# Reading three quarters of unit 0's turned rows during the MLP, and loading the output weights later

## The chip, the cores and the metric

The kernel runs on one core of a Trainium2 chip. The metric is the device time of one execution in microseconds, as the median of several runs. All matrices are fp32; products that need accuracy are made of two fp32r parts, a high one and a low one. Engine names below are those of the profile: PE (TensorE matmuls), PEld (its weight loads), DVE (VectorE), ACT (ScalarE), POOL (GpSimd) and SP (SyncE, which here only issues DMAs).

## The reference

One sequence of S = 2048 tokens, width D = 448, is normalised; attention with 16 heads of 28 and one shared key and value head, and a GELU MLP of width 1792, both work on the normalised rows, and both are added to the input:

```python
xn = _layernorm(x, axis=-1)
# attention
q = (xn @ wq).reshape(B, S, H, Dh).transpose(0, 2, 1, 3); k = xn @ wk; v = xn @ wv
p = softmax(einsum("bhqd,bkd->bhqk", q, k) * Dh ** -0.5)
a = einsum("bhqk,bkd->bhqd", p, v).transpose(0, 2, 1, 3).reshape(B, S, H * Dh) @ wo
# MLP, with a layernorm of its own
h = gelu(einsum("bsd,df->bsf", _layernorm(xn), w1) + b1)
return x + a + einsum("bsf,fd->bsd", h, w2) + b2
```

## The kernel before

The schedule is written out by hand: every engine runs its instructions in the order in which the Python code issues them, and the tile framework adds the waits. Three stages follow each other.

**Projections** (to about 64 us). The tokens are worked in four chunks of 512. Each chunk's normalised and transposed rows stand in two tiles of 128 x 2048, the *row buffers*: `xh` (the high part, pool `xt_p`, three buffers) and `xl` (the low part, pool `xl_p`, three buffers).

**MLP** (64 to 481 us). 56 slots: four chunks (`c`, in the order 1, 2, 3, 0) by 14 blocks of F (`ft`). A slot takes some 7.4 us. Between the MLP's products PE also makes score products, three PSUM banks in turn (`mtile`), of two kinds:

- the *max stream* (L598): scores whose row maxima DVE takes (L599);
- the *turned scores* (L632): for one head of each unit, DVE scales and copies the scores of 128 queries into one of two `raw` buffers (L633), ACT takes the exponential (L650), and SP stores the quarter of a head with four DMAs of 256 KB to DRAM, `td<-raw` (L653). The next but one quarter can be written into the same `raw` buffer only when those four DMAs have landed.

**Attention** (481 us to the end). 16 units (512 queries by four heads), each of 8 steps of two key blocks `kt`. Three heads of a unit go by `score` (a product L1037, then the exponential on ACT, L1038). The fourth is the turned one: its rows come back from DRAM by `load_d` (L830, `half<-td`), a *half* tile being 8 key blocks, 256 columns, brought by four DMAs of 32 partitions each; `turn_blocks` (L1013) then turns two key blocks at a time with one DVE transpose of 128 x 1024. The products with the values are `pv` (L999). The strings in `ORDERS` set the order within two steps: `s` a score, `m` a product of the max stream, `t` a turned score, `x` an exponential of turned scores with its stores, `T` a transpose of turned rows, a digit that many `pv`. `begin(n)` stands at the head of step n: it issues the loads for the next unit (`load_d(u + 1, kt // 2)` on SP, `load_q` on POOL).

Unit 0's turned rows are 16 key blocks, four quarters of four. Quarter 0 is read in the MLP's last chunk into a free `xh` row buffer called `ahead` (L788, one DMA of 256 KB in each of the slots 6 to 9). Quarter 1 (L1079, four DMAs of 256 KB) and quarters 2 and 3 (L1081, four DMAs of 512 KB) are issued at the start of the attention stage, behind the four DMAs of the output weights `wor` (L853). These weights are set to zero by POOL (L850), loaded, and split into `woh` (ACT, L856) and `wol` (POOL, L857) by `prep_wo` in steps 4 to 7. They are used by `o_jobs` (L874 to L876) from 674 us on, and `wor` itself at the very end (L950). All three stand in the pool `att`, which is opened when the MLP's pools are closed.

SP issues in order: a DMA that waits (for an engine, or for the eighth DMA before it) holds all that stand behind it.

Of the kernel before, what the change touches and what calls it, by code (L numbers as in the profile page):

```python
# [10 lines left out]
F32 = mybir.dt.float32  # L11
# [31 lines left out]
def block_kernel(ctx, tc, x, wq, wk, wv, wo, w1, b1, w2, b2, out):  # L43
# [4 lines left out]
    def f(t):  # L48
        return t.bitcast(F32)
# [5 lines left out]
    dram = ctx.enter_context(tc.tile_pool(name="dram", bufs=1, space=bass.MemoryType.DRAM))  # L55
    xt_p = ctx.enter_context(tc.tile_pool(name="xt", bufs=len(KEPT)))
    qmp = ctx.enter_context(tc.tile_pool(name="qmp", bufs=1))

    def heads_of(u):
        return 4 - sum(v == u for v, _ in TURNED)  # L60
# [11 lines left out]
    ident = keep.tile([P, P], F32, name="ident")  # L72

    ph1 = ExitStack()
    xl_p = ph1.enter_context(tc.tile_pool(name="xl", bufs=len(KEPT)))
    wp = ph1.enter_context(tc.tile_pool(name="wp", bufs=1))
    lnp = wp.tile([P, NT, 2], F32, name="lnp")
    lnrq = wp.tile([P, 2, NT], F32, name="lnrq")
# [488 lines left out]
        qst.append(xt_p.tile([P, 4, CW], F32R, name="xh"))  # L567
        pool.memset(f(qst[-1]), 0.0)

    qst = []  # L570

    mrs = {}

# [191 lines left out]
    for n in range(len(mslots) + 2):  # L765
        c, ft = mslots[n] if n < len(mslots) else (NCH, n - len(mslots))
        if 3 <= ft < 11 and ft % 2 and len(KEPT) <= c + 1 < NCH:
            line(CT * MLP_ORDER[c + 1] + (ft - 3) // 2)
        k = ft - (10 if c < NCH - 1 else 5)
        if c < NCH and 0 <= k < CT:  # L770
            line(CT * MLP_ORDER[c] + k)
        if c < NCH and 0 < k <= CT:
            a = lines[CT * MLP_ORDER[c] + k - 1]
            pool.tensor_add(a, a, b2b)
        if ft == 0 and 0 < c < NCH:
            a = lines[CT * MLP_ORDER[c - 1] + CT - 1]
            pool.tensor_add(a, a, b2b)
        if (c, ft) == (NCH - 1, 4):
            clear_q()
        if c == NCH - 1 and 6 <= ft < 10:  # L780
            load_q(0, (ft - 6,))
        if (c, ft) == (NCH - 1, 11):
            load_max(0)
        if (c, ft) == (NCH - 1, 5):
            ahead = f(xt_p.tile([P, 4, CW], F32R, name="xh")).rearrange("p b n -> p (b n)").rearrange("p (t k) -> p t k", k=P)
        if c == NCH - 1 and 6 <= ft < 10:
            r = ft - 6
            nc.sync.dma_start(ahead[32 * r:32 * r + 32], td[0, 3][:, r, :, 0:P])  # L788
        ts, pace = 0, 21
        if n == 2:  # L790
            pace = 20
        if 0 < c < NCH:
            pace += {1: -2, 2: -2, 4: 2, 6: 2}.get(ft, 0)
        if n >= len(mslots):
            done = 0
        for _ in slot(n):
            done += 1
            owed += pace
            if n >= len(mslots) and (done % 2 if ft == 0 else done <= 2):
                maxed += mxs.step()  # L800
            elif 0 < n < len(mslots) and owed // 46 > (owed - pace) // 46:
                if n == 1 and ts == 0:
                    ts += tq.step()
                elif ts < 4 and n < len(mslots) - 1 and not split(c, ft):
                    ts += tq.step()
                else:
                    maxed += mxs.step()
        if n == 0:
            for _ in range(3):
                tq.step()  # L810
# [5 lines left out]
    op = ctx.enter_context(tc.tile_pool(name="op", bufs=1, space=PSUM))  # L816
    free_at.update((i, k) for k, i in enumerate((0, 1, 6, 3, 2, 4, 5)))

    wor = att.tile([P, NG, D], F32, name="wor", bufs=1)
    halves = {}  # L820

    def load_d(u, i, at=slice(0, 256)):
        assert stored[u, 3] == CT - 1
        h, r = divmod(i, 4)
        if (u, 3, h) not in halves:
            halves[u, 3, h] = att.tile([P, 4 * CT, 256], F32, name="half", bufs=3)
        part = halves[u, 3, h][32 * r:32 * r + 32]
        if u:
            dve.memset(part[0:1, 0, 0:1], 0.0)
        nc.sync.dma_start(part[:, :, at], td[u, 3][:, r, :, 256 * h + at.start:256 * h + at.stop])  # L830
# [14 lines left out]
        part = part[32 * r:32 * r + 32]  # L845
        nc.sync.dma_start(part, td[u, j][:, r, :, P * q:P * q + P])

    woh = att.tile([P, NG, D], F32R, name="woh", bufs=1)
    wol = att.tile([P, NG, D], F32R, name="wol", bufs=1)
    pool.memset(wor, 0.0)  # L850
    for j in range(4):
        src = wo.rearrange("(g j d) n -> j d g n", j=4, d=DH)[j]
        nc.sync.dma_start(wor[32 * j + 1:32 * j + 1 + DH, :, :], src)  # L853

    def prep_wo(g):
        act.activation(woh[:, g, :], wor[:, g, :], AF.Copy)  # L856
        pool.tensor_sub(wol[:, g, :], wor[:, g, :], f(woh[:, g, :]))  # L857

# [148 lines left out]

    def turn_blocks(u, kt, j):
        p = pair_of()
        part, k = (halves[u, j, kt // 8], kt % 8) if j == 3 else (halves[u, j, kt // 4], kt % 4)  # L1010
        if u == 0 and kt < 4:
            part = ahead
        dve.transpose(p.rearrange("p k (g j) -> p g k j", j=32),  # L1013
                      part[:, :, 32 * k:32 * k + 64].rearrange("p g (k j) -> p g k j", j=32))
        ps[u, kt, j], ps[u, kt + 1, j] = p[:, 0], p[:, 1]
        taken[id(p), 0], taken[id(p), 1] = (u, kt), (u, kt + 1)
# [39 lines left out]
    def begin(n):  # L1056
# [13 lines left out]
        if u == NU - 1 and kt < 4:  # L1070
            for r in range(4):
                load_second(2 + kt // 2, r)
        if 4 <= n < 4 + NG:
            prep_wo(n - 4)
        if u + 1 < NU and kt < 8:
            load_q(u + 1, (kt // 2,))

    for i in range(4):
        load_d(0, i, slice(P, 2 * P))  # L1079
    for i in range(4, 8):  # L1080
        load_d(0, i)  # L1081
    for n0 in range(0, len(steps), 2):
        u, kt0 = steps[n0]
        n, kt = n0, kt0
# [78 lines left out]
```

## Time and profile before

| what | us |
|---|---|
| median of 3 runs (lowest to highest) | 1078.3 (1077.69 to 1078.35) |
| the profiled execution | 1077.61 |
| its span, first to last instruction | 1075.8 |
| PE busy | 1058.8 (98%) |
| DVE, ACT, POOL busy | 914.1 (85%), 723.9 (67%), 563.2 (52%) |
| mean granted TensorE clock | 0.996 |
| moved by DMA | 209.86 MB, mean 195 GB/s |

The lines quoted in the prediction come from these views. *Windows* give for stretches of the span the busy time of each engine with its number of instructions, then the granted TensorE clock (1.00 is full), the busy share of the 16 DMA engines (it can exceed 1) and the GB/s moved. *Timeline* rows have start, duration, engine, line, operation and tiles; a bracket at the end is the idle time of that engine before the row and what ended it. The *chain* is the work that ended last, followed back from a stretch's end: start, duration, what. *Waits* give who waited for whom: total, times, longest. *DMA issues* give count and size of each.

### The profile page before, as it was taken

To read this page: it belongs to the slowest core of one execution; us is meant where nothing else is said; L and a number is where in the kernel's file an instruction comes from. 1 tells how busy PE (TensorE), PEld (TensorE's weight loads), DVE (VectorE), ACT (ScalarE), POOL (GpSimd) and SP (SyncE) were. 2 spreads that over 40 slices of the span, in tenths; PEclk is the share of its full clock that TensorE was granted. 3 is DMA by queue.
4 is the path that set the end of the run, shared out by engine and by line. 5 is a ranking of instruction groups with operands and counts; after the bars stand their busy time and mean duration, and the time that the engine had idled before them with its cause. 6 is when DMAs were issued, how large, how long until landed. Compare 5 with 4: busy or idle time off the path is not lost.

```text
span 1075.8 us, 17796 instructions
## 1 busy us (share of the span) xinstructions
PE 1058.8 (98%) x5805; PEld 714.2 (66%) x5805; DVE 914.1 (85%) x1880; ACT 723.9 (67%) x1240; POOL 563.2 (52%) x704
## 2 busy tenths in 40 slices
PE   9999999999999999998899999999999999999998
PEld 8778888888888888884445455655545644556455
DVE  7889999999999999996788888788888787776755
ACT  6775456565566656545778888678887687775773
POOL 6678787768766777773333434335333335343130
PEclk9999999999999999999999999999999999999999
DMA  8865556668776777859999999999999797896892
GB/s 266 249 220 149 136 133 167 160 169 202 189 188 168 183 190 211 222 142 218 234 221 217 236 211 245 215 191 236 220 227 239 188 222 175 170 189 150 185 213 57
DMA packets 158768, 209.86 MB, mean 195 GB/s; under 512 B 17950, under 2 KB 110276, under 8 KB 158676
## 3 DMA queue, kind: packets, MB, share of 16 engines
q1 hardware_dynamic: 146132, 187.28, 71.7%
q0 software_dynamic: 11136, 20.87, 9.3%
q8 instruction: 46, 0.75, 0.3%
q10 hardware_dynamic: 1408, 0.57, 0.2%
q14 instruction: 46, 0.38, 0.1%
HBM read 121.31 MB, written 86.10 MB: 193 GB/s over the span
## 4 chain that ended last, share of the span: by engine, by line
PE 93%; DMA 2%; DVE 2%; ACT 2%; issue 1%; SPq 0%; POOL 0%; ACTq 0%; DVEq 0%; POOLq 0%
PE po L999 19%; PE m L1037 17%; PE m L598 16%; PE m L715 12%; PE ph L192 11%; PE m L632 6%; PE qp L192 3%; PE ph L195 1%; PE m L874 1%; PE ph L197 1%; PE m L876 1%; PE m L875 1%; DMA half<-td 1%; DMA td<-raw 1%; ACT p L1038 1%; PE po L982 1%
## 5 line engine op out<-in xcount | busy, mean ns | idle before, releaser
L599 DVE TENSOR_REDUCE mx<-m 128x1 f32<-128x512 f32 x752 | 484.7, 682 | 73.7 <-PE m L598 69.7
L1038 ACT ACTIVATE p<-m 128x512 f32<-128x512 f32 x652 | 342.4, 623 | 112.2 <-PE m L1037 109.4
L598 PE MATMUL m<-ks,qm 128*128 128x512 f32 x752 | 289.4, 400 | 4.1 <-DVE raw L633 3.0
L1037 PE MATMUL m<-xh,ks 128*128 128x512 f32 x752 | 261.4, 416 | 4.8 <-DVE mx L599 4.3
L999 PE MATMUL po<-p,vs 128*32 128x512 f32 x1664 | 219.5, 595 | 0.9 <-DVE p L1013 0.9
L1037 PEld LDWEIGHTS m<-xh,ks 128*128 128x128 f32 x752 | 139.1, 189 | 100.9 <-issue 40.8
L633 DVE TENSOR_SCALAR_CACHE_REDUCE raw<-m 128x512 f32<-128x512 f32 x272 | 181.7, 687 | 12.7 <-PE m L632 6.1
L598 PEld LDWEIGHTS m<-ks,qm 128*128 128x128 f32 x752 | 141.9, 189 | 43.8 <-issue 11.7
L650 ACT ACTIVATE raw<-raw,m 128x1024 f32<-128x1024 f32 x136 | 153.0, 1163 | 0.0
L680 ACT ACTIVATE hx<-ph,b1t 128x512 f32<-128x512 f32 x55 | 37.9, 688 | 150.5 <-PE ph L197 98.9
L1013 DVE STREAM_TRANSPOSE p<-half 128x1024 f32<-128x1024 f32 x112 | 137.8, 1234 | 1.5 <-DMA half<-td 1.1
L999 PEld LDWEIGHTS po<-p,vs 128*32 128x32 f32 x1664 | 55.0, 109 | 108.7 <-issue 105.3
L632 PE MATMUL m<-ks,q 128*128 128x512 f32 x272 | 108.1, 398 | 0.1
L696 POOL TENSOR_TENSOR hl<-hx,hh 128x512 fp32r<-128x512 f32 x56 | 72.7, 1298 | 32.4 <-ACT hh L694 32.3
L715 PE MATMUL m<-w2h,hl 128*128 128x448 f32 x224 | 81.4, 367 | 0.0
L715 PE MATMUL m<-w2h,hh 128*128 128x448 f32 x224 | 81.3, 366 | 0.0
L715 PE MATMUL m<-w2l,hh 128*128 128x448 f32 x224 | 81.2, 366 | 0.0
L684 POOL TENSOR_TENSOR hz<-hz,hx 128x512 f32<-128x512 f32 x56 | 72.8, 1300 | 4.6
L689 POOL TENSOR_TENSOR hx<-hx,hz 128x512 f32<-128x512 f32 x56 | 72.7, 1297 | 4.7
L1038 ACT ACTIVATE xh<-m 128x512 f32<-128x512 f32 x100 | 55.9, 624 | 21.5 <-PE m L1037 21.0
L192 PE MATMUL ph<-xh,w1h 128*128 128x512 f32 x165 | 64.7, 392 | 0.0
L999 PE MATMUL po<-xh,vs 128*32 128x512 f32 x256 | 64.7, 595 | 0.0
(197 smaller groups left out, 1499.7 us busy)
## 6 DMA issues: line engine op xcount, KB each, us to landing
td<-raw SPq DMA_DIRECT2D x272, 256.0 KB
half<-td SPq DMA_DIRECT2D x124, 512.0 KB
xh<-qd POOLq DMA_DIRECT2D x56, 168.0 KB, 6.9
qd<-qe SPq DMA_DIRECT2D x24, 256.0 KB
a<-in_A_x_dram SPq DMA_DIRECT2D x24, 224.0 KB
qm<-qd SPq DMA_DIRECT2D x96, 56.0 KB
qm<-qd POOLq DMA_DIRECT2D x92, 56.0 KB, 5.8
ad<-a SPq DMA_DIRECT2D x16, 224.0 KB
```

Source lines behind the costliest of these rows:

```text
L192: pe.matmul(ps, w, v, start=(n == 0), stop=False)
L598: pe.matmul(pm, qm[:, t * P:(t + 1) * P], ks[:, n * CW:(n + 1) * CW], start=True, stop=True)
L599: dve.tensor_reduce(mx[:, CT * j + t, n:n + 1], pm, axis=AX.X, op=ALU.max)
L632: pe.matmul(sc, q3[i % 2][:, t * P:(t + 1) * P], ks[:, n * CW:(n + 1) * CW], start=True, stop=True)
L633: dve.tensor_scalar(raw[:, :, 4 * n:4 * n + 4, :].rearrange("p r b i -> p b r i"), sc.rearrange("p (b r i) -> p b r i", r=4, i=32), SCALE, ...
L650: act.activation(raw[:, rs], raw[:, rs], AF.Exp, bias=m3[:, 4:5], scale=1.0)
L684: pool.tensor_mul(hz, hz, hx)
L715: pe.matmul(m2[k], h[:, k * P:(k + 1) * P], w[:, ft, :], start=(ft == 0 and i == 0), stop=(ft == NF - 1 and i == 2))
L999: pe.matmul(po[32 * j:32 * j + 32, :], vs[:, kt, :], ps.pop((u, kt, j)), start=(kt == 0), stop=(kt == NT - 1))
L1013: dve.transpose(p.rearrange("p k (g j) -> p g k j", j=32), part[:, :, 32 * k:32 * k + 64].rearrange("p g (k j) -> p g k j", j=32))
L1037: pe.matmul(s, ks[:, kt * P:(kt + 1) * P], qss[u][:, j, :], start=True, stop=True)
L1038: act.activation(p, s, AF.Exp, scale=SCALE)
```

## The change

- The pool of `xl` row buffers is opened at the top, so it lives to the end; the pool of the MLP's weights and others after it move up in memory accordingly.
- `ahead` becomes a list of three row buffers, one `xh` and two `xl`, for quarters 0, 1 and 2 of unit 0's turned rows. They are read by twelve DMAs of 256 KB, two in each of the slots 6 to 11 of the MLP's last chunk.
- At the start of the attention stage only quarter 3 is left to read (four DMAs of 256 KB).
- `wor`, `woh`, `wol` are `xl` row buffers. `wor`'s four loads are issued one each in steps 4 to 7; the split is in steps 10 to 13.

```diff
+    xl_p = ctx.enter_context(tc.tile_pool(name="xl", bufs=len(KEPT)))
...
-    xl_p = ph1.enter_context(tc.tile_pool(name="xl", bufs=len(KEPT)))
...
         if (c, ft) == (NCH - 1, 5):
-            ahead = f(xt_p.tile([P, 4, CW], F32R, name="xh")).rearrange("p b n -> p (b n)").rearrange("p (t k) -> p t k", k=P)
-        if c == NCH - 1 and 6 <= ft < 10:
-            r = ft - 6
-            nc.sync.dma_start(ahead[32 * r:32 * r + 32], td[0, 3][:, r, :, 0:P])
+            for p, name in ((xt_p, "xh"), (xl_p, "xl"), (xl_p, "xl")):
+                t = f(p.tile([P, 4, CW], F32R, name=name)).rearrange("p b n -> p (b n)")
+                ahead.append(t.rearrange("p (t k) -> p t k", k=P))
+        if c == NCH - 1 and 6 <= ft < 12:
+            for i in (2 * ft - 12, 2 * ft - 11):
+                q, r = divmod(i, 4)
+                nc.sync.dma_start(ahead[q][32 * r:32 * r + 32], td[0, 3][:, r, :, P * q:P * q + P])
...
-    wor = att.tile([P, NG, D], F32, name="wor", bufs=1)
+    def weights_tile():
+        t = xl_p.tile([P, 4, CW], F32R, name="xl").rearrange("p b n -> p (b n)")
+        return t[:, 0:NG * D].rearrange("p (g d) -> p g d", g=NG)
+
+    wor = f(weights_tile())
...
-    woh = att.tile([P, NG, D], F32R, name="woh", bufs=1)
-    wol = att.tile([P, NG, D], F32R, name="wol", bufs=1)
     pool.memset(wor, 0.0)
-    for j in range(4):
+    woh = wol = None
+
+    def load_wo(j):
         src = wo.rearrange("(g j d) n -> j d g n", j=4, d=DH)[j]
         nc.sync.dma_start(wor[32 * j + 1:32 * j + 1 + DH, :, :], src)
 
     def prep_wo(g):
+        nonlocal woh, wol
+        if g == 0:
+            woh, wol = weights_tile(), weights_tile()
...
-        part, k = (halves[u, j, kt // 8], kt % 8) if j == 3 else (halves[u, j, kt // 4], kt % 4)
-        if u == 0 and kt < 4:
-            part = ahead
+        if u == 0 and kt < 12:
+            part, k = ahead[kt // 4], kt % 4
+        elif j == 3:
+            part, k = halves[u, j, kt // 8], kt % 8
+        else:
+            part, k = halves[u, j, kt // 4], kt % 4
...
-        if 4 <= n < 4 + NG:
-            prep_wo(n - 4)
+        if 4 <= n < 8:
+            load_wo(n - 4)
+        if 10 <= n < 10 + NG:
+            prep_wo(n - 10)
...
-    for i in range(4):
+    for i in range(4, 8):
         load_d(0, i, slice(P, 2 * P))
-    for i in range(4, 8):
-        load_d(0, i)
```

PE's and DVE's instructions stand in the same order as before; SP's, POOL's and ACT's differ. On SP, in the slots 9 to 11 of the MLP's last chunk, before (`xh<-qd` is unit 0's queries, `q` and `qm` queries for coming scores, `mn` unit 0's maxima):

```order
L563 DMA xh<-qd_90 28x3x512
L788 DMA xh<-td_3_73 32x16x128
L498 DMA q_162<-qd_90 28x512 x2
L498 DMA q_162<-qd_91 28x512 x2
L653 DMA td_3_84<-raw 128x1x512 x8
L498 DMA qm_161<-qd_90 28x512 x2
L498 DMA qm_161<-qd_91 28x512 x2
L585 DMA xh<-mn 1x12x128
L586 DMA xh<-mn 1x12x128
L653 DMA td_3_84<-raw 128x1x512 x8
```

And now:

```order
L563 DMA xh<-qd_94 28x3x512
L791 DMA xl<-td_3_76 32x16x128 x2
L498 DMA q_162<-qd_93 28x512 x2
L498 DMA q_162<-qd_94 28x512 x2
L653 DMA td_3_87<-raw 128x1x512 x4
L791 DMA xl<-td_3_76 32x16x128 x2
L653 DMA td_3_87<-raw 128x1x512 x4
L498 DMA qm_161<-qd_93 28x512 x2
L498 DMA qm_161<-qd_94 28x512 x2
L585 DMA xh<-mn 1x12x128
L586 DMA xh<-mn 1x12x128
L791 DMA xl<-td_3_76 32x16x128 x2
```

Each pair of new reads stands ahead of the four (in the last case eight) stores of turned scores of its slot. In the slots 6 to 9 one read became two, in 10 and 11 none became two.

On SP at the start of the attention stage, before:

```order
L721 DMA ad<-a 128x448 x4
L853 DMA wor<-in_A_wo_dram 28x4x448 x4
L830 DMA half<-td_3_73 32x16x128 x4
L830 DMA half<-td_3_73 32x16x256 x4
L830 DMA half<-td_3_74 32x16x256 x7
L653 DMA td_3_85<-raw 128x1x512 x4
```

And now (`xl<-in_A_wo_dram` are the output weights; `td_3_76` is unit 0's turned head, `td_3_77` unit 1's):

```order
L721 DMA ad<-a 128x448 x4
L837 DMA half<-td_3_76 32x16x128 x4
L837 DMA half<-td_3_77 32x16x256 x5
L860 DMA xl<-in_A_wo_dram 28x4x448
L837 DMA half<-td_3_77 32x16x256
L860 DMA xl<-in_A_wo_dram 28x4x448
L837 DMA half<-td_3_77 32x16x256
L860 DMA xl<-in_A_wo_dram 28x4x448
L653 DMA td_3_88<-raw 128x1x512 x4
```

Ahead of the first store of turned scores of this stage there stood 4 weight loads, 4 reads of 256 KB and 11 of 512 KB; now 3 weight loads, 4 reads of 256 KB and 7 of 512 KB.

On DVE, unit 0's second and third transposes (`xh` as a source is quarter 0's row buffer, `xh` as a target a spare one for the turned result), before and now:

```order
L1013 STREAM_TRANSPOSE p<-xh 128x16x2x32
L829 MEMSET half 1x1
L599 TENSOR_REDUCE mx<-m_5705 128x1
L1013 STREAM_TRANSPOSE xh<-half 128x16x2x32
L599 TENSOR_REDUCE mx<-m_5712 128x1
```

```order
L1026 STREAM_TRANSPOSE p<-xh 128x16x2x32
L836 MEMSET half 1x1
L599 TENSOR_REDUCE mx<-m_5703 128x1
L1026 STREAM_TRANSPOSE xh<-xl 128x16x2x32
L599 TENSOR_REDUCE mx<-m_5710 128x1
```

The third transpose stands at the same place and reads a row buffer that the MLP's last chunk filled, where it read a half tile that the attention stage's first DMAs fill.

More of the change, by code (lines that the diff above doesn't have):

```diff
@@ L568, in clear_q @@
         pool.memset(f(qst[-1]), 0.0)
-    qst = []
+    qst, ahead = [], []
     mrs = {}
```

## The prediction

> **What bounds the kernel now.** I read the windows first, to see in which stage PE is not busy.
>
> ```profile
> 66.00:421.00 355.00, 353.91 (x1604) 298.17 (x1603) 339.65 (x742) 209.55 (x292) 268.86 (x263) 1.00 0.66 169
> 421.00:450.00 29.00, 29.00 (x134) 24.74 (x133) 27.43 (x63) 16.85 (x24) 23.17 (x23) 1.00 0.87 247
> 450.00:481.00 31.00, 31.00 (x144) 26.45 (x143) 30.16 (x60) 14.49 (x21) 21.33 (x21) 1.00 0.52 127
> 481.00:545.00 64.00, 55.25 (x291) 29.17 (x289) 47.04 (x94) 44.38 (x85) 22.52 (x32) 0.95 1.08 232
> 545.00:1030.00 485.00, 485.00 (x2912) 257.81 (x2912) 392.55 (x757) 371.94 (x701) 177.48 (x288) 1.00 0.92 207
> ```
>
> The columns after the stretch are PE, PEld, DVE, ACT, POOL, the clock, the DMA share and GB/s. PE is the bound everywhere but in the first 64 us of attention: there it is idle for 64 - 55.25 = 8.75 us and its mean clock falls to 0.95, with the DMA engines at 1.08. The timeline of PE has these gaps:
>
> ```profile
> 481.97 0.50 PE L1037 MATMUL m<-xh,ks 128*128 128x512 f32 x1 [0.49 <-DVE half L829]
> 488.90 1.90 PE L999 MATMUL po<-p,vs 128*32 128x512 f32 x10 [0.88 <-DVE p L1013]
> 500.01 0.73 PE L1037 MATMUL m<-xh,ks 128*128 128x512 f32 x2 [4.28 <-DVE mx L599]
> 531.45 0.70 PE L598 MATMUL m<-ks,qm 128*128 128x512 f32 x1 [2.99 <-DVE raw L633]
> ```
>
> They add up to 8.64 us, so these four are the whole story. DVE's timeline says what DVE itself waited for ahead of the two large ones:
>
> ```profile
> 498.13 1.25 DVE L1013 STREAM_TRANSPOSE xh<-half 128x1024 f32<-128x1024 f32 x1 [5.93 <-DMA half<-td]
> 530.69 0.69 DVE L633 TENSOR_SCALAR_CACHE_REDUCE raw<-m 128x512 f32<-128x512 f32 x1 [3.35 <-DMA td<-raw]
> ```
>
> The first is unit 0's third transpose, which waits for quarter 1; while DVE stands, it frees no PSUM bank, and PE runs out of banks. The second is a turned score that waits until its `raw` buffer has been stored. Narrow windows show what follows a gap:
>
> ```profile
> 486.00:496.00 10.00, 8.86 (x48) 3.34 (x47) 5.32 (x9) 5.29 (x12) 1.50 (x4) 1.00 1.11 210
> 496.00:500.00 4.00, 0.00 (x0) 0.00 (x0) 1.82 (x2) 0.00 (x0) 0.30 (x1) 1.00 1.14 216
> 500.00:505.00 5.00, 4.88 (x13) 3.65 (x14) 4.50 (x12) 3.53 (x7) 3.73 (x8) 0.66 1.13 221
> ...
> 531.00:536.00 5.00, 4.55 (x13) 3.46 (x13) 4.90 (x10) 2.83 (x6) 0.88 (x2) 0.66 1.09 182
> ```
>
> After each large gap the clock is 0.66 over 5 us, so PE loses 5 x 0.34 = 1.70 us more; after the gaps of 0.49 and 0.88 it is full (1.00 in 486 to 496). And the DMA engines are saturated at 210 to 221 GB/s. The chain names the two DMAs that ended last:
>
> ```profile
> 485.96 12.00 DMA half<-td
> ...
> 515.83 1.03 ACT raw L650
> ...
> 519.39 11.11 DMA td<-raw
> ```
>
> A read of 256 KB took 12.00 us and a store of 256 KB 11.11 us, because of what is queued ahead of them.
>
> **The change, part by part.** *The first gap.* Quarter 1 is now in a row buffer that was filled in the MLP, so the third transpose follows the second at once (about 492 instead of 498.13). That returns 4.28 + 1.70 = **5.98 us**. Late next is DVE: between its wait and PE's next value products it has up to 4.5 us of work in 5 us (the row of 500 to 505), while PE's 4.88 us there shrink to 3.2 at full clock. Since DVE then starts 5.93 us earlier, it has that much lead, and I allow 0.4 us for what PE may still wait (between 0, if the lead lasts, and 1.3, the difference 4.5 - 3.2).
>
> *The second gap.* The first store of the attention stage had 4 weight loads (196 KB), 4 reads of 256 KB and 11 of 512 KB ahead of it on SP, 7.62 MB; now it has 3, 4 and 7, 5.32 MB. At 221 GB/s the 2.30 MB less are 10.4 us of queue. But all of it also happens 5.98 us earlier, so that the queue has less time to drain. Rows for the time that is left:
>
> ```profile
> 516.89 3.75 SPq L653 DMA_DIRECT2D td<-raw  x4
> xh<-qd POOLq DMA_DIRECT2D x56, 168.0 KB, 6.9
> ```
>
> In the attention stage a load of 168 KB takes 6.9 us to land (median); I take this for a store in an ordinary queue. The last store (issued at 519.39) took 11.11, 4.2 us more; 4.2 + 5.98 = 10.2 us of queue have to go, and 10.4 go. The store would then land 2.5 (from the first issue, 516.89, to the last) + 6.9 = 9.4 us after the exponential; DVE comes for the buffer at 530.69 - 3.35 = 527.34, which is 10.48 us after the exponential's end at 516.86, and both shift alike. It fits by 1.1 us, so I count the gap as gone: 2.99 + 1.70 = **4.69 us**, between 0 (the queue is no shorter when it counts) and 4.69. That the steady stretch from 545 on runs with PE at 485.00 of 485.00 under the same stores and reads of 512 KB speaks for the upper end.
>
> On the clock, the Trainium skill ("TensorE: Matmul & The Clock Gate", section "What's actually happening") puts the return to half rate after an idle window of about 3.4 us. By it the gap of 2.99 would have left the clock alone, and this term would be 2.99; the row of 531 to 536 shows 0.66, and the row decides.
>
> *The gaps of 0.49 and 0.88* stand in front of any moved data (quarter 0 was already early). I keep them; if POOL's earlier `memset` freed them, 1.37 us more would go.
>
> *The eight added reads in the MLP's last chunk* (twelve now, four before), in stretches of about a slot:
>
> ```profile
> 421.00:428.00 7.00, 7.00 (x34) 5.98 (x33) 6.64 (x16) 3.92 (x6) 5.84 (x6) 1.00 0.89 255
> 428.00:435.00 7.00, 7.00 (x34) 5.96 (x33) 6.70 (x17) 3.91 (x7) 5.75 (x7) 1.00 0.86 248
> 435.00:442.00 7.00, 7.00 (x33) 5.96 (x32) 6.63 (x16) 4.11 (x7) 6.12 (x6) 1.00 0.82 250
> 442.00:449.00 7.00, 7.00 (x33) 5.97 (x33) 6.55 (x16) 3.91 (x7) 5.11 (x5) 1.00 0.92 237
> 449.00:456.00 7.00, 7.00 (x34) 5.86 (x33) 6.83 (x18) 4.00 (x6) 5.11 (x5) 1.00 0.60 146
> 456.00:463.00 7.00, 7.00 (x34) 5.96 (x33) 6.75 (x16) 4.07 (x6) 5.12 (x5) 1.00 0.55 136
> 428.04 0.40 SPq L788 DMA_DIRECT2D xh<-td  x1
> DVE raw L633 <- PE m L632: 0.6, 2, 0.3
> ```
>
> Saturation being 1.11, the room is 0.22, 0.25, 0.29 and 0.19 of 7 us in the first four, 1.54, 1.75, 2.03 and 1.33 us (6.65 together), and 3.57 and 3.92 us in the last two (7.49). A read of 262,144 bytes at 221 GB/s costs 1.19 us, one more in each of the first four, two more in the last two: it fits everywhere, and SP's 0.40 us of issue is hidden while SP waits for ACT's exponentials. But each read stands ahead of its slot's four stores, and the `raw` buffers are only two: DVE's L633 waits for the store of the quarter before last, and behind L633 on DVE stand the reductions that free PE's three banks. From 395 to 480 DVE waits at L633 for PE alone of any account (the last row), so the stores land in time now; how much slack they have no view shows. Ends: 0, and 8 x 1.19 = 9.5 us if each added microsecond became a wait. I take **0.6 us**, half a read, once: the room in each stretch exceeds the read.
>
> That price holds if time goes by bytes. If it goes by rows (the new reads bring 512 bytes a row, the halves 1 KB), a read costs as much as a half's 512 KB, 2.37 us. The row of 486 to 496, in which the 512-byte reads of quarter 1 move among others at 210 GB/s, against 216 to 221 for halves alone, is far nearer to bytes.
>
> *The weights.* Four loads of 0.2 MB (0.91 us each at 221 GB/s) move behind the urgent reads, and are counted above. The split moves from steps 4 to 7 to steps 10 to 13:
>
> ```profile
> L856 ACT ACTIVATE woh<-wor x4: 571/616/654, 504.7 to 517.2; 128x448 fp32r<-128x448 f32 x4
> L857 POOL TENSOR_TENSOR wol<-wor,woh x4: 1154/1164/1167, 509.6 to 517.9; 128x448 fp32r<-128x448 f32 x4
> 545.00:673.00 128.00, 128.00 (x774) 64.58 (x774) 111.73 (x227) 105.93 (x196) 53.60 (x87) 1.00 1.00 225
> ```
>
> ACT gets 0.62 us in each of four steps of some 4.4 us in which it is 83% busy, POOL 1.16 where it is 42% busy; their users come at 674. Behind them stand ACT's exponentials and POOL's loads for the next units. Ends: 4 x 0.62 = 2.5 us lost or, as ACT is freed of them in unit 0, gained. I take 0, the slack in each step being 0.75 us.
>
> *Sum*, on the profiled execution: 1077.6 - 5.98 - 4.69 + 0.4 + 0.6 = 1067.9. The median of the runs stands 0.7 above that execution, so **1068.6 us**. From 545 on PE is at 100%, so nothing there can take the gain back.
>
> **Rivals.**
>
> *The store's wait stays*: the margins above are 0.2 us of queue and 1.1 us of landing, both from medians. Then only the first gap goes: 1077.6 - 5.98 + 1.0 + 0.7 = 1073.3. For it speak the saturated DMA engines until 545 (1.08); against it the 2.30 MB.
>
> *Time goes by rows*, 2.37 us a read: the overflow beyond the room is 0.83 + 0.62 + 0.34 + 1.04 in the first four stretches and 1.17 + 0.82 in the last two, 4.8 us; in place of the 0.6 it gives 1072.8. Against it: 210 GB/s.
>
> *Slower: the stores of turned scores fall behind in the MLP.* At p us a read, the overflow is 8p - 14.1 us, all of it DVE waiting at L633 and PE behind it. It eats the whole gain and 2.2 us more from p = 3.3; at 4 us, a rate of 66 GB/s, it is 17.9, and the time 1077.6 - 10.3 + 17.9 + 0.7 = 1085.9. Only the 12.00 us of the chain's read, which stood behind seven other DMAs, looks like that; the 0.87 share at 247 GB/s, with one such read a slot, speaks against it.
>
> The Trainium skill ("SBUF — State Buffer", section "The DMA setup-cost knee") gives every transfer about 2 us that do not scale with bytes, and advises the largest single transfer; the change cuts four reads of 512 KB into eight of 256 KB. Its formula, 2 + bytes / 436 GB/s, makes a read 2.6 us (an estimate from that page); if these added up one after the other, p = 2.6 would give 8p - 14.1 = 6.7 us and 1074.7. The row of 486 to 496 shows them overlapping, so I give this 3 in 100.
>
> *The change doesn't do what it says*: the row buffers are not free in slot 6, or another wait takes the third transpose's place. The buffers were last read a whole chunk earlier, in slots 28 to 41. Time: 1078.3.
>
> **How the numbers follow.** Forecast 0.66, with a range of its own from 1066.3 (the small gaps go too, and nothing is lost in the MLP) to 1070.5 (about 2 us lost in the MLP or at DVE). The store's wait stays 0.17, rows 0.05, the page's fixed cost 0.03, slower 0.05, no effect 0.04. What a measurement can tell from no change is 0.2%, 2.2 us. Faster: 0.66 + 0.17 + 0.05 + 0.03 = 0.91; same 0.04; slower 0.05. The range reaches from 1066.3 to 1073.5, which takes in the first two rivals and leaves out what lies above.
>
> **What would show it.** Right: on DVE the third transpose, from `xl`, has no wait for a DMA; PE has no gap over 2 us and a clock of 1.00 from 481 to 545; PE stays at 100% from 421 to 481; the DMA share rises to about 1.0 there and falls below 1.08 behind it. Wrong: a wait of L633 for `td<-raw` at some 521 us (the first rival), or such waits between 430 and 463 (the others); or PE waiting for ACT at 540 to 560, where the split now stands.

## The result and the profile after

| what | before | after |
|---|---|---|
| median (lowest to highest), us | 1078.32 (1077.69 to 1078.62) | 1068.73 (1067.37 to 1071.26) |
| the profiled execution, us | 1077.61 | 1067.84 |
| its span, us | 1075.8 | 1066.1 |

The ratio is 0.9915, 95% interval 0.9894 to 0.9935: faster by 9.6 us, where 9.7 were forecast (1068.6).

Windows of the changed kernel, with the columns of the prediction (PE, PEld, DVE, ACT, POOL, clock, DMA share, GB/s), and behind them the last one before the change:

```profile
421.00:450.00 29.00, 28.89 (x132) 24.38 (x131) 26.42 (x62) 16.44 (x24) 22.71 (x23) 1.00 1.00 265
450.00:481.00 31.00, 31.00 (x144) 26.55 (x143) 30.18 (x61) 14.73 (x21) 23.28 (x23) 1.00 0.65 178
490.00:545.00 55.00, 55.00 (x327) 27.71 (x326) 47.31 (x95) 46.37 (x88) 18.65 (x30) 1.00 1.07 227
```

```profile
490.00:545.00 55.00, 47.62 (x255) 25.23 (x253) 38.66 (x78) 38.29 (x73) 16.69 (x26) 0.94 1.10 230
```

From 490 to 545 us PE is busy throughout at full clock, where before it was busy for 47.62 of 55 us, with the DMA engines nearly as full as before (1.07 and 1.10). In the MLP's last chunk the share rose from 0.87 to 1.00 and from 0.52 to 0.65, and PE lost 0.11 us there (28.89 of 29.00). Of PE's gaps in the first 64 us of the attention stage the two small ones are left:

```profile
482.18 0.50 PE L1050 MATMUL m<-xh,ks 128*128 128x512 f32 x1 [0.55 <-DVE half L836]
489.10 1.90 PE L1009 MATMUL po<-p,vs 128*32 128x512 f32 x10 [0.88 <-DVE p L1026]
```

On DVE's timeline, unit 0's third transpose (now from `xl`) and the first turned score that needs a stored buffer have no bracket, so DVE waited for neither; a new wait stands in the MLP (third row). The bracket names a product that runs in every slot; what ended the wait is the store: the product that L633 reads had ended at 444.87, and the last piece of the store `td<-raw` landed at 445.76:

```profile
492.31 1.23 DVE L1026 STREAM_TRANSPOSE xh<-xl 128x1024 f32<-128x1024 f32 x1
521.36 0.68 DVE L633 TENSOR_SCALAR_CACHE_REDUCE raw<-m 128x512 f32<-128x512 f32 x1
446.27 0.69 DVE L633 TENSOR_SCALAR_CACHE_REDUCE raw<-m 128x512 f32<-128x512 f32 x1 [1.34 <-PE ph L192]
```

Where the 9.7 us of span came from can be read by marking the same two products in both kernels: the one behind the small gap at the start of the attention stage (481.97 before, 482.18 after) and a late one of the last unit, here before and after. Two more pairs of the same product, counted in PE's order, split the way between the marks (rows of the table):

```profile
1040.92 0.41 PE L982 MATMUL po<-p,vs 128*32 128x256 f32 x2 [0.32 <-DVE p L1013]
```

```profile
1030.92 0.41 PE L992 MATMUL po<-p,vs 128*32 128x256 f32 x2 [0.32 <-DVE p L1026]
```

| stretch | before | after | change |
|---|---|---|---|
| to the first mark | 481.97 | 482.18 | +0.21 |
| first gap: to the product at 520.10 (514.23 after) | 38.13 | 32.05 | -6.08 |
| second gap: to the product at 559.90 (549.66 after) | 39.80 | 35.43 | -4.37 |
| to the second mark | 481.02 | 481.26 | +0.24 |
| between the marks, together | 558.95 | 548.74 | -10.21 |
| from the second mark to the end | 34.88 | 35.18 | +0.30 |

Of what was gained, 0.54 us are given back behind 560 us, nearly all of it behind 970; the cause stays open.

### The profile page after: what moved, and what is told of

Same layout as the page of the kernel before. It is cut to its first block, busy times and chain, and to the rows that moved or that the text cites. A ratio compares the mean times of both kernels' runs of the same rounds, so it can differ in the third digit from the quotient of the medians.

```text
span 1066.1 us, 17806 instructions
## 1 busy us (share of the span) xinstructions
PE 1055.8 (99%) x5805; PEld 711.8 (67%) x5805; DVE 912.5 (86%) x1880; ACT 723.2 (68%) x1240; POOL 561.8 (53%) x704
## 4 chain that ended last, share of the span: by engine, by line
PE 94%; DVE 3%; DMA 1%; ACT 1%; issue 0%; SPq 0%; ACTq 0%; DVEq 0%
PE po L1009 19%; PE m L1050 18%; PE m L598 16%; PE m L715 12%; PE ph L192 11%; PE m L632 6%; PE qp L192 3%; DVE mx L599 1%; PE ph L195 1%; PE m L884 1%; PE ph L197 1%; PE m L885 1%; PE m L886 1%; DMA raw<-td 1%; PE po L992 1%; PE m L992 1%
## 5 line engine op out<-in xcount | busy, mean ns | idle before, releaser
L633 DVE TENSOR_SCALAR_CACHE_REDUCE raw<-m 128x512 f32<-128x512 f32 x272 | 181.4, 687 | 10.1 <-PE m L632 5.8
L1026 DVE STREAM_TRANSPOSE p<-half 128x1024 f32<-128x1024 f32 x110 | 135.3, 1234 | 0.4
L563 POOL DMA_DIRECT2D xh<-qd x60 | 37.6, 628 | 62.7 <-PE m L1050 40.8
L682 POOL TENSOR_SCALAR hz<-hz 128x512 f32<-128x512 f32 x56 | 34.8, 622 | 57.4 <-ACT hz L681 57.1
```

Of the source, the lines that this page charges most:

```text
L633: dve.tensor_scalar(raw[:, :, 4 * n:4 * n + 4, :].rearrange("p r b i -> p b r i"), sc.rearrange("p (b r i) -> p b r i", r=4, i=32), SCALE, ...
L1026: dve.transpose(p.rearrange("p k (g j) -> p g k j", j=32), part[:, :, 32 * k:32 * k + 64].rearrange("p g (k j) -> p g k j", j=32))
```

## The experiments

The prediction's theory: one saturated queue of DMAs carries reads, weights and stores, and what counts for a wait is the bytes ahead. Quarter 1's early read removes the first gap; the second goes because quarters 1 and 2 no longer stand ahead of the first store. The rivals give the gain to the weights, or to quarter 1 alone, or price a read otherwise. All diffs are against the changed kernel.

| kernel | median (lowest to highest), us | ratio to before (95%) |
|---|---|---|
| weights alone | 1080.25 (1078.36 to 1080.83) | 1.0022 (1.0012 to 1.0031) |
| two quarters | 1072.94 (1072.84 to 1075.75) | 0.9959 (0.9943 to 0.9974) |
| weights first | 1068.44 (1067.21 to 1069.68) | 0.9912 (0.9896 to 0.9929) |
| four reads a slot | 1076.64 (1074.12 to 1079.50) | 0.9990 (0.9978 to 1.0001) |
| as changed, again | 1067.16 (1066.60 to 1067.55) | 0.9895 (0.9881 to 0.9910) |
| reads in slots 8 to 13 | 1066.30 (1066.06 to 1067.11) | 0.9889 (0.9877 to 0.9902) |
| the same, again | 1067.88 (1067.51 to 1069.14) | 0.9910 (0.9897 to 0.9922) |
| reads cut in two | 1070.51 (1069.20 to 1071.39) | 0.9925 (0.9913 to 0.9937) |
| weights in steps 8 to 11 | 1073.14 (1067.73 to 1074.93) | 0.9951 (0.9931 to 0.9970) |
| both late | 1069.66 (1066.91 to 1072.79) | 0.9918 (0.9902 to 0.9934) |
| both late, again | 1070.42 (1067.42 to 1072.61) | 0.9932 (0.9917 to 0.9948) |
| reads late, weights first | 1067.15 (1066.14 to 1068.22) | 0.9901 (0.9888 to 0.9914) |

The first four shared a chip, and so did the groups (as changed, slots 8 to 13, both late, cut in two) and (the four others); before was 1077.49, 1078.27 and 1078.16 there.

### The weights alone

```diff
-            for p, name in ((xt_p, "xh"), (xl_p, "xl"), (xl_p, "xl")):
+            for p, name in ((xt_p, "xh"),):
-        if c == NCH - 1 and 6 <= ft < 12:
-            for i in (2 * ft - 12, 2 * ft - 11):
+        if c == NCH - 1 and 6 <= ft < 10:
+            for i in (ft - 6,):
-        if u == 0 and kt < 12:
+        if u == 0 and kt < 4:
-    for i in range(4, 8):
-        load_d(0, i, slice(P, 2 * P))
+    for i in range(4):
+        load_d(0, i, slice(P, 2 * P))
+    for i in range(4, 8):
+        load_d(0, i)
```

> Only the weights are moved (loads in steps 4 to 7, split in steps 10 to 13, in row buffers); the turned rows are read as before (quarter 0 alone in the MLP). Theory of the prediction (reads and stores pass through one saturated queue, so that what counts is the bytes ahead): quarter 1 lands 0.8 MB / 221 GB/s = 3.6 us sooner, DVE waits some 2.3 us for it in place of 5.93, and PE's first gap falls from 4.28 to about 0.7. But the first store has only one weight load (0.2 MB, 0.9 us) less ahead of it and lands at about 529.6 in place of 530.5, while DVE comes some 5 us sooner: DVE waits about 8 us at the turned score of the attention stage, the second gap grows to some 7 us, and the time is 1077.3 us, a gain of one microsecond. Rival (the weights at the head of the queue were what made both waits): both gaps go, 1069 to 1070 us.

Measured: 1080.25, slower than before. PE's gaps over 0.6 us (the first four rows), DVE's waits for DMAs, and SP's issue of the first store:

```profile
488.87 1.90 PE L1009 MATMUL po<-p,vs 128*32 128x512 f32 x10 [0.87 <-DVE p L1026]
496.38 0.73 PE L1050 MATMUL m<-xh,ks 128*128 128x512 f32 x2 [0.69 <-DVE mx L599]
507.17 0.50 PE L1050 MATMUL m<-xh,ks 128*128 128x512 f32 x1 [1.40 <-DVE mx L599]
533.71 0.79 PE L598 MATMUL m<-ks,qm 128*128 128x512 f32 x1 [7.95 <-DVE raw L633]
494.50 1.25 DVE L1026 STREAM_TRANSPOSE xh<-half 128x1024 f32<-128x1024 f32 x1 [2.34 <-DMA half<-td]
505.29 1.25 DVE L1026 STREAM_TRANSPOSE p<-half 128x1024 f32<-128x1024 f32 x1 [2.87 <-DMA half<-td]
532.96 0.69 DVE L633 TENSOR_SCALAR_CACHE_REDUCE raw<-m 128x512 f32<-128x512 f32 x1 [8.30 <-DMA td<-raw]
516.03 5.79 SPq L653 DMA_DIRECT2D td<-raw  x4
```

The first wait came out as worked out beforehand (2.34 us on DVE and a gap of 0.69; 2.3 and 0.7 expected). Behind it stands one that was not expected, for quarter 2 (2.87 us on DVE and a gap of 1.40 on PE). What the first wait returned was swallowed by these two: 8.30 us at the store. So the weights at the head did delay quarter 1, but taking them away brings nothing while the first store stays where it is. The size was off: DVE went on at 532.96 and not at about 529.6. The windows from 481 to 530.5 of the kernel before and of this one show why in part:

```profile
481.00:530.50 49.50, 41.70 (x225) 21.40 (x223) 34.52 (x67) 34.65 (x65) 19.50 (x27) 0.97 1.09 236
```

```profile
481.00:530.50 49.50, 41.06 (x224) 19.81 (x222) 34.39 (x67) 32.90 (x61) 12.96 (x22) 0.97 1.08 226
533.00:538.00 5.00, 4.29 (x10) 3.41 (x11) 4.80 (x10) 2.47 (x5) 0.00 (x0) 0.50 0.99 185
```

At nearly the same share the engines moved 226 GB/s in place of 236; over 49.5 us that is 0.5 MB, or 2.2 us of queue, more than the 0.9 us that one weight load less was worth. The store was also issued late. Its exponential ended at 513.20, but SP, which issues in order, reached the first of its four DMAs at 516.03 and the last at 521.26; in the kernel before it went from 516.89 to 519.39, right behind the exponential's end at 516.86. Why the rate is lower, and which of the two comes first, isn't settled. The second row of this kernel adds that the clock stayed at 0.50 for 5 us after the long gap, where 0.66 had been the mean after the gaps of before.

### Two quarters instead of three

```diff
-            for p, name in ((xt_p, "xh"), (xl_p, "xl"), (xl_p, "xl")):
+            for p, name in ((xt_p, "xh"), (xl_p, "xl")):
-        if c == NCH - 1 and 6 <= ft < 12:
+        if c == NCH - 1 and 6 <= ft < 10:
-        if u == 0 and kt < 12:
+        if u == 0 and kt < 8:
-        load_d(0, i, slice(P, 2 * P))
+        load_d(0, i)
```

> As the change, but only quarters 0 and 1 are read in the MLP (eight reads, slots 6 to 9); quarters 2 and 3 are read at the start of the attention stage as four DMAs of 512 KB, as before. Theory of the prediction: the first gap stays away (quarter 1 is there); the first store of the attention stage has 1.05 MB more ahead of it, 4.7 us at 221 GB/s, lands at about 525.4 and DVE, which comes for the buffer at 521, waits about 4 us; PE has a gap of 3 to 4 us there, its clock falls to about 0.66 over the next 5 us (1.7 us), and the time is 1073 to 1074 us. Rival (quarter 1 alone is what counts, the second gap was a late echo of the first): no such wait, 1068 to 1069 us.

Measured: 1072.94. PE's one large gap, DVE's wait behind it, and the windows around:

```profile
526.85 0.66 PE L598 MATMUL m<-ks,qm 128*128 128x512 f32 x1 [4.39 <-DVE raw L633]
526.10 0.69 DVE L633 TENSOR_SCALAR_CACHE_REDUCE raw<-m 128x512 f32<-128x512 f32 x1 [4.75 <-DMA td<-raw]
500.00:505.00 5.00, 5.00 (x40) 2.31 (x33) 3.72 (x8) 3.30 (x7) 0.93 (x2) 1.00 1.13 218
527.00:532.00 5.00, 5.00 (x17) 3.47 (x21) 4.85 (x10) 3.47 (x7) 0.63 (x1) 0.66 0.99 198
```

The first gap is gone with quarter 1 alone (500 to 505 us: 5.00 at full clock). The second is back: 1.05 MB more ahead of the store are 4.75 us at 221 GB/s, and DVE waited 4.75 us. That the two agree to the digit is chance: counted from the product behind the small gap at the stage's start, the store landed 5.42 us later than in the change, and there it had 0.66 us in hand (table further below). This splits the gain: on this chip 4.6 us (1077.49 to 1072.94) come with two quarters, and the third brings 4.5 more (to 1068.44, next kernel), through the store's queue and not through its own transposes.

### The weights at the head again

```diff
-        if 4 <= n < 8:
-            load_wo(n - 4)
...
+    for j in range(4):
+        load_wo(j)
     for i in range(4, 8):
```

> As the change, but the four loads of the weights stand at the head of the attention stage's DMAs as before; the split stays in steps 10 to 13. Theory of the prediction: quarter 3 lands 3.6 us later, at about 498.7 for its last read, still ahead of its first transpose at 509.6; the first store has 0.2 MB more ahead of it and lands 0.9 us later, which is about what it had in hand: 1068.7 to 1069.6 us, where the small end means no wait and the large end a wait of under 1 us. Rival (the later loading of the weights carries part of the gain of its own): the wait of DVE for quarter 3 or for the store is back with some 3.6 us, 1072 us or more.

Measured: 1068.44 against 1068.73 for the change in its first runs: the same. There is no gap in the first 64 us of the attention stage but the two small ones, so loading the weights later carries none of the gain, and with 0.2 MB more ahead of it the first store is still in time. It was not 0.9 us later, as expected, but landed 1.34 us earlier, counted in the same way. What PE lost in this kernel's profile stands in the MLP, which is the same code as in the change:

```profile
455.88 0.50 PE L632 MATMUL m<-ks,q 128*128 128x512 f32 x1 [0.85 <-DVE raw L633]
455.13 0.69 DVE L633 TENSOR_SCALAR_CACHE_REDUCE raw<-m 128x512 f32<-128x512 f32 x1 [1.54 <-PE ph L192]
438.26 0.69 DVE L633 TENSOR_SCALAR_CACHE_REDUCE raw<-m 128x512 f32<-128x512 f32 x1 [0.42 <-DMA td<-raw]
```

The wait sits at other slots than in the profile after (455 here, 446 there), and once its releaser is named as the store. The stores in the MLP's last chunk are just in time, sometimes late.

### Four reads a slot

```diff
-        if c == NCH - 1 and 6 <= ft < 12:
-            for i in (2 * ft - 12, 2 * ft - 11):
+        if c == NCH - 1 and 6 <= ft < 9:
+            for i in range(4 * ft - 24, 4 * ft - 20):
```

> As the change, but the twelve reads of the MLP's last chunk stand four in each of the slots 6 to 8, where the DMA engines have the least room, and none in 9 to 11. Theory of the prediction (time goes by bytes, and a read in excess of the room delays the stores behind it): three reads more than the kernel before in each slot are 3 x 1.19 = 3.57 us against a room of 1.54, 1.75 and 2.03 us, an excess of 5.4 us at the end of slot 8; less what the stores have in hand, DVE waits at the turned scores 2 to 5 us between 430 and 463, PE loses as much, and the time is 1071 to 1074 us. Rival 1 (the price is by rows, 2.37 us a read): an excess of some 16 us, 1080 us or more. Rival 2 (reads anywhere in the chunk are hidden, since the mean share of the chunk stays below 1.1): 1068.7 us.

Measured: 1076.64; nearly the whole gain is gone. DVE's waits, PE's largest gap, and two windows:

```profile
433.26 0.69 DVE L633 TENSOR_SCALAR_CACHE_REDUCE raw<-m 128x512 f32<-128x512 f32 x1 [2.74 <-DMA td<-raw]
442.12 0.69 DVE L633 TENSOR_SCALAR_CACHE_REDUCE raw<-m 128x512 f32<-128x512 f32 x1 [1.95 <-PE ph L192]
453.27 0.69 DVE L633 TENSOR_SCALAR_CACHE_REDUCE raw<-m 128x512 f32<-128x512 f32 x1 [4.84 <-DMA td<-raw]
454.02 0.80 PE L632 MATMUL m<-ks,q 128*128 128x512 f32 x1 [3.85 <-DVE raw L633]
421.00:450.00 29.00, 26.51 (x119) 21.79 (x117) 22.28 (x51) 15.22 (x22) 21.74 (x22) 1.00 1.04 252
452.52:459.34 6.82, 5.32 (x13) 4.47 (x14) 4.50 (x12) 2.72 (x4) 1.28 (x2) 0.50 0.60 174
```

This is the slower rival's mechanism at work: 9.5 us of waiting at L633 in three slots, and a clock of 0.50 over 6.82 us around the end of the longest. It lies above the 2 to 5 us of the price by bytes and below the 16 of the price by rows. Nine reads beyond the kernel before took up the room of 5.3 us and 9.5 us more: (5.3 + 9.5) / 9 = 1.65 us each, an estimate that leaves out what the stores had in hand. The idea that reads are hidden by the mean share of the chunk is out: where in the chunk they stand is worth 8 us.

### The reads later, once more as changed, and cut in two

Reads in the slots 8 to 13 (run twice, on two chips), with the change beside them:

```diff
-        if c == NCH - 1 and 6 <= ft < 12:
-            for i in (2 * ft - 12, 2 * ft - 11):
+        if c == NCH - 1 and 8 <= ft < 14:
+            for i in (2 * ft - 16, 2 * ft - 15):
```

> The changed kernel as it is, once more beside the others of this call: 1068.7 us, in single runs 1067 to 1071 as before. Theory: the spread comes from the MLP's last chunk, where the stores land so narrowly ahead of the turned scores that waits of 0.3 to 1.5 us on DVE come and go; the profile shows such waits at L633 between 430 and 460, and none for the store in the attention stage. Rival: it comes from the first store of the attention stage, which has about as little in hand; then the profile of a run above 1069 shows the wait there, with a gap and a lower clock.

> As the change, but the twelve reads stand two in each of the slots 8 to 13 of the MLP's last chunk; slots 10 to 13 have more room (share 0.60, 0.83 and 0.36 from 456 us on in the changed kernel). Theory (the reads ahead of the stores cost what PE loses in the MLP, 0.1 to 0.9 us, and make the spread): DVE's waits at L633 in slots 6 to 9 fall to under 0.5 us, PE has no gap from 421 to 481, the time is 1067.5 to 1068.2 us, and single runs lie within about 1 us. Rival (the reads now finish too late, or the place of the reads doesn't matter): 1068.7 us or more, with a wait for unit 0's first turned rows at 488 us.

> The change with its twelve reads in the slots 8 to 13, once more beside the others of this call: 1066 to 1067 us, single runs within about 1 us, no wait of DVE for a store that costs PE anything.

Measured: as changed 1067.16, with a gap of 0.49 us on PE at 447.76 for L633 (first row); slots 8 to 13 on the same chip 1066.30, without a gap from 421 to 481; on the other chip 1067.88, with a gap of 0.44 there (second row), where 1066 to 1067 and no such gap had been expected:

```profile
447.76 0.50 PE L632 MATMUL m<-ks,q 128*128 128x512 f32 x1 [0.49 <-DVE raw L633]
```

```profile
455.26 0.50 PE L632 MATMUL m<-ks,q 128*128 128x512 f32 x1 [0.44 <-DVE raw L633]
```

The intervals of the ratios overlap, and the waits can still come: a gain from the later slots isn't shown. The slowest run of the change (1071.26, mean clock 0.998, so with a long gap somewhere) had no like in four more, and no profile caught it: its cause stays open.

The reads cut in two, same bytes and rows in twice the DMAs:

```diff
-                nc.sync.dma_start(ahead[q][32 * r:32 * r + 32], td[0, 3][:, r, :, P * q:P * q + P])
+                for t in (0, 8):
+                    nc.sync.dma_start(ahead[q][32 * r:32 * r + 32, t:t + 8], td[0, 3][:, r, t:t + 8, P * q:P * q + P])
```

> As the change, but each of the twelve reads of the MLP's last chunk is two DMAs of 128 KB (8 blocks of the 16), four in each slot; bytes and rows are the same. Theory (time goes by bytes): the engines' share stays, SP issues 12 DMAs more at 0.4 to 0.5 us each, in part while it waits anyway: 1068.7 to 1070 us. Rival (each DMA costs a fixed time on the engines): with 2 us each, 24 us over six slots, four in each: DVE waits several us at L633 as with four reads of 256 KB a slot, 1074 us or more.

Measured: 1070.51, 3.35 us more than as changed on the same chip; the intervals are apart. It lies between what the theory and the rival gave. PE's two gaps, and SP's issue of one slot's reads and of the stores behind them, in this kernel and then as changed:

```profile
448.12 0.50 PE L632 MATMUL m<-ks,q 128*128 128x512 f32 x1 [1.26 <-DVE raw L633]
457.66 0.50 PE L632 MATMUL m<-ks,q 128*128 128x512 f32 x1 [1.40 <-DVE raw L633]
438.05 1.85 SPq L792 DMA_DIRECT2D xl<-td  x4
440.01 3.43 SPq L653 DMA_DIRECT2D td<-raw  x4
```

```profile
436.99 0.85 SPq L791 DMA_DIRECT2D xl<-td  x2
437.95 3.89 SPq L653 DMA_DIRECT2D td<-raw  x4
```

So a DMA has a price besides its bytes, 3.35 / 12 = 0.28 us each at the kernel's end here. It shows at SP: four reads take it 1.85 us to issue where two took 0.85, and the stores behind them go out 2.06 us later by this slot. On the DMA engines it hardly shows: from 421 to 485 us their share is 0.80 at 211 GB/s, and as changed 0.82 at 222. The Trainium skill ("SBUF — State Buffer", section "The DMA setup-cost knee") is right in its direction, fewer and larger transfers; its 2 us do not add up one after the other in this kernel.

### The weights later still

Loads in steps 8 to 11, the split in steps 14 to 17; alone, and together with the reads in slots 8 to 13 ("both late", run twice):

```diff
-        if 4 <= n < 8:
-            load_wo(n - 4)
-        if 10 <= n < 10 + NG:
-            prep_wo(n - 10)
+        if 8 <= n < 12:
+            load_wo(n - 8)
+        if 14 <= n < 14 + NG:
+            prep_wo(n - 14)
```

> Reads in slots 8 to 13, and the weights' loads in steps 8 to 11 with the split in steps 14 to 17. Theory: the loads of the weights do not bear on any wait that is left, since with all four of them ahead the first store was not late either; so the same as with the reads moved alone, 1067.5 to 1068.2 us. Rival (the store of the attention stage is what spreads the runs): 0.5 us or more faster than with the reads moved alone, and no run above 1068.

> As the change (reads in slots 6 to 11), but the weights are loaded in steps 8 to 11 and split in steps 14 to 17. Theory A (these loads stand ahead of the second store of the attention stage, at about 528 us, and make it late in some runs; that is where the kernel with both edits got runs of up to 1072.8 with a mean clock of 0.997): the same spread, runs between 1067 and 1073, the slower ones with a clock of 0.998 or less. Theory B (the spread of that kernel came from somewhere else, the reads in slots 8 to 13 or the chip): runs like those of the change, 1066.6 to 1069, all with a clock of 0.999 or 1.0.

> Reads in slots 8 to 13 and the weights in steps 8 to 11, once more. Theory A (weights' loads ahead of the second store): runs between 1067 and 1073 again; if the profiled one is above 1069, DVE waits for td<-raw at L633 at about 541 us, with a gap of over 2 us on PE. Theory B (chance of that call): 1066 to 1067.5 us throughout.

Measured: 1069.66 and 1070.42 with both, 1073.14 alone, in runs from 1066.91 to 1074.93. I had expected no effect, and that was wrong; so was theory A's mechanism. The profile of the weights alone in these steps fell on a run of 1074.48. PE's gap, the window behind it, and DVE's waits from 545 to 600 us:

```profile
564.71 0.47 PE L598 MATMUL m<-ks,qm 128*128 128x512 f32 x1 [2.86 <-DVE p L1026]
565.00:570.00 5.00, 5.00 (x30) 1.29 (x32) 0.86 (x3) 0.60 (x1) 0.00 (x0) 0.66 1.06 200
DVE mx L599 <- PE m L598: 10.2, 6, 5.4
```

DVE waits for no store there, only for PE. The gap is at a product of the max stream, which reads `qm`, and `qm` is loaded by POOL. POOL's timeline ahead of it, in this kernel and in the one with reads in slots 8 to 13 (second run), whose split stands in steps 10 to 13:

```profile
549.08 1.29 POOL L925 TENSOR_TENSOR oc<-oc,tr 128x512 f32<-128x512 f32 x1 [7.39 <-DMA tr<-ld]
550.33 1.16 POOL L867 TENSOR_TENSOR xl<-xl 128x448 fp32r<-128x448 f32 x1
551.46 0.61 POOL L931 TENSOR_SCALAR oth<-oc 128x512 fp32r<-128x512 f32 x1
552.16 1.29 POOL L932 TENSOR_TENSOR otl<-oc,oth 128x512 fp32r<-128x512 f32 x1
553.39 2.06 POOL L498 DMA_DIRECT2D qm<-qd  x4
DMA to landing us min/median/max: 5.1/6.6/9.6
```

```profile
546.50 1.27 POOL L925 TENSOR_TENSOR oc<-oc,tr 128x512 f32<-128x512 f32 x1 [4.31 <-DMA tr<-ld]
549.79 2.06 POOL L498 DMA_DIRECT2D qm<-qd  x4
DMA to landing us min/median/max: 4.0/5.4/6.6
```

The four `qm` loads are issued 3.6 us later: POOL waits longer for its own `tr<-ld`, and then has 1.16 us of the split ahead of them. The last one goes out at 554.93 and takes 9.6 us (last row of each, issue to landing). It landed at 564.51, PE goes on at 564.71, and what PE waited for there were the semaphores of these four loads. So the name in the bracket, DVE, had nothing to do with it. In the profiles with both late, of runs of 1066.91 and 1068.69, the same product waits 0.47 and 0.89 us and starts 0.2 us behind the landing of its last `qm` load (560.73 and 562.51), as it does here. In the other kernel the last `qm` load landed at 557.65, 6.86 us earlier. Of these, 1.16 are the split on POOL; 5.2 are slower landings, of `tr<-ld` by 1.9 and of `qm` by 3.3, while the DMA engines were fuller (1.03 from 545 to 550 us, against 0.79). That the weights' later loads are what filled them is likely, but no run moved the loads without the split.

### The reads later, the weights first

```diff
         if c == NCH - 1 and 8 <= ft < 14:
...
-        if 4 <= n < 8:
-            load_wo(n - 4)
+    for j in range(4):
+        load_wo(j)
```

> Reads in the slots 8 to 13, the weights' loads at the head of the attention stage as before the change, the split in steps 10 to 13. Theory A (the weights' place at the head costs nothing, since quarter 3 is needed at 509 us and the first store has enough in hand): 1066 to 1067 us, as with the reads moved alone, little spread. Rival (moving the weights behind the reads matters once the MLP's waits are gone): 1067.5 us or more, with a wait for the first store at 521 us.

Measured: 1067.15, where the change had 1067.16 in its second set of runs: again it makes no difference whether the weights are loaded at the head or in steps 4 to 7. In its profile, of a run of 1068.22, PE loses 2.0 us once between 545 and 1030 us to an exponential, so that some of the spread of single runs isn't the MLP's:

```profile
PE m L1050 <- ACT p L1051: 2.0, 1, 2.0
```

No version that was run is clearly faster than the change.

## Why the prediction was right, point by point

- **First gap, 5.98 us**: right. The third transpose has no wait, PE and its clock are full from 490 on. Two quarters alone show it, too.
- **Second gap, 4.69 us**: right that it goes, and for the reason given; it returned 4.37. The margin was smaller than worked out. The traces record when the last piece of a DMA has landed. For the first store of the attention stage, counted from the first mark, the product behind the small gap at 482 us:

  | kernel | MB ahead of the store | landed after, us | in hand when DVE came, us |
  |---|---|---|---|
  | before | 7.62 | 48.53 | -3.16 |
  | weights alone | 7.42 | 50.89 | -8.16 |
  | two quarters | 6.37 | 43.94 | -4.61 |
  | weights first | 5.52 | 37.18 | 2.06 |
  | the change | 5.32 | 38.52 | 0.66 |

  The store came 10.0 us earlier in the change, where the prediction's working gave 10.2 (the 5.98, and 4.2 us less to land), and had 0.66 us in hand, where 1.1 had been worked out: its last DMA took 8.1 us to land, and 6.9 had been taken for it from loads of another size. The quarters thus follow the price by bytes to within a microsecond. The weights do not: 0.2 MB more ahead came 1.34 us earlier, 0.2 MB less 2.36 later. The same store in other profiles of the changed order landed after 37.7 to 39.4 us, so 0.2 MB can't be read from single profiles; the 3.3 us by which it missed in the kernel with the weights alone are more than that.
- **What PE may still wait for DVE, 0.4 us**: PE waits for nothing from 490 to 545, so this is 0 by the window.
- **The sum**: the two gaps returned 10.45 us, where 5.98 + 4.69 - 0.4 = 10.27 were forecast for them. That the end agrees to 0.1 us is in part luck. The allowances of 0.4 and 0.6 us were hardly used in the profile after (0 and 0.11), and instead 0.54 us were lost behind 560, where the prediction had said that nothing could be. The two clock terms of 1.70 were right (last section: 3.41 us at half the clock, 1.71).
- **Small gaps**: kept, right (0.55 and 0.88).
- **Added reads in the MLP, 0.6 us**: right in kind and size. PE lost 0.11 us in the profile after, and 0.49, 0.85 and 0.88 in three other profiles with the same reads. They wait where it was said, at L633 between 430 and 463. The price by bytes, 1.19 us a read, was too low: about 1.65 in the four-a-slot run, an estimate that takes in what the issue on SP costs. At two a slot the room still covers most of that.
- **The weights, 0**: right for the steps 10 to 13, and for a reason that is narrower than the one given. I bounded it by ACT's 0.62 us a step; what loads and split cost four steps later comes through PE's `qm` loads, which POOL issues behind the split (1.16 of 6.86 us) and which land later (most of the rest).
- **Rivals**: the store's wait stays (1073.3) is what the kernel with two quarters does (1072.94). The slower one is what four reads a slot do. The rival of a fixed price of 2 us for each transfer falls with the reads cut in two.

## What to carry to other kernels

When a full DMA queue feeds two waits, removing the first alone can lengthen the second and lose: ask for each moved byte which later store or load stands behind it. A read moved into another stage costs by the slot it lands in, not by the stage's mean share. When work or loads are moved, ask also whose loads stand behind them on the issuing engine and in the DMA queue. The name in a wait's bracket must be tested against the DMA that the waiting product reads.

## What was not expected of the hardware

What a gap of PE costs behind itself does not follow from its length. Over the next 5 us the clock was 0.66 after gaps of 2.86, 2.99, 4.28 and 4.39 us, but 0.50 after 3.85 (four reads a slot) and 7.95 (the weights alone), and it stayed full after 0.88, 1.40, 1.62 (four reads a slot) and 2.0 (reads late, weights first).

The clock changes in the traces show why. The stretches at half the clock last 3.413 us (behind four of these gaps), 6.83 (behind 3.85) and 10.24 (behind 7.95): one, two and three times 3.413. In the kernel before, the clock fell at 500.86 and at 531.58 us, 30.72 us apart, which is nine times 3.413. So in these traces the clock is set anew every 3.413 us, at times that do not depend on when a gap begins. Three such stretches in a row, in the kernel before:

```profile
494.03:497.44 3.41, 1.70 (x10) 0.88 (x6) 0.00 (x0) 1.22 (x3) 0.55 (x1) 1.00 1.13 198
497.44:500.86 3.42, 0.74 (x3) 0.31 (x3) 2.64 (x5) 0.32 (x1) 0.00 (x0) 1.00 1.12 217
500.86:504.27 3.41, 3.41 (x8) 2.73 (x9) 2.98 (x7) 2.48 (x6) 3.00 (x6) 0.50 1.12 222
```

And the one ahead of the fall with the weights in steps 8 to 11:

```profile
562.79:566.20 3.41, 1.49 (x10) 0.58 (x14) 3.08 (x5) 2.09 (x3) 0.00 (x0) 1.00 1.04 172
```

The gap of 4.28 us left PE busy for 1.70 us of the first of these stretches and for 0.74 of the second, and the clock fell behind the second alone. In all profiles here it fell behind every full-clock stretch with at most 1.49 us of PE's work, and behind none with 1.70 or more. So what counts is how much of one stretch a gap leaves idle, and with it how the gap falls across the borders. Each stretch at half the clock that PE fills costs 1.71 us. Behind 3.85 us there were two: the gap reached 1.50 us into the first, which left PE busy for 1.91 us of it.

The Trainium skill ("TensorE: Matmul & The Clock Gate", section "What's actually happening") gives half the clock after an idle window of about 3.4 us, and says that the window is free-running. The traces agree in the length (3.413 us) and in the fixed times; but the window did not have to be idle throughout (PE was busy for 1.49 of its 3.41 us), and that is why gaps of 2.86 and 2.99 us were enough.
